# Weight rows 68 KB apart in DRAM instead of 64 KB: a gap of 4 KB behind every row of a load

## The chip, the cores and the metric

The kernel runs on one core of one Trainium2 chip. The metric is the device time of one execution in microseconds. Times are medians of several runs. The profile comes from one further execution.

## The reference

One decode step of a transformer block for 8 sequences: layer norm, attention over the last 1024 cached positions (32 query heads, 4 key and value heads, head size 128), a residual sum, a second layer norm, a gated MLP (1024 to 3584 to 1024), and a second residual sum. All in float32.

```python
q = (_layernorm(x) @ wq)                       # [8, 1, 32*128]
k = k_cache[:, :, Sk - W:, :]                  # W = 1024 of Sk = 4096, each head used by 8 query heads
v = v_cache[:, :, Sk - W:, :]
h = x + (softmax(q @ k.T * Dh ** -0.5) @ v) @ wo
n = _layernorm(h)
h2 = h + (gelu(n @ w_gate) * (n @ w_up)) @ w_down
```

With one token for each sequence nearly all the work is to bring the weights and the two caches from DRAM to the core: 111.2 MB, each byte used once.

## The kernel before

The host packs weights and caches into one flat DRAM array, `weights`. It is made of 20 parts, one for each load. A part is a matrix of 128 rows, one for each partition, and a row holds all that this partition gets from the load. Eleven parts have rows of 64 KB (16384 float32: the two halves of wq, K, V, wo, and three of the gate and up matrices), three have rows of 32 KB, two of 16 KB, one of 8 KB, one of 4 KB, and two of 2 KB. Rows and parts lie one behind the other without a gap, so the distance between two rows of a part is the length of a row.

In SBUF the array `w` has two buffers of 64 KB a partition, `wbuf[0]` and `wbuf[1]`, filled in turn. The function `load` (the issue stands on L186) starts loads 0 to 15 from the SP queue; the list `flow` gives each one's buffer, its offset and its source. Load k waits until TensorE has finished the products that read the same buffer before (`pe(...)`, two stages back). The last four loads, the `tail` (rows of 8, 4, 2 and 2 KB), go through `move` (L83). All 20 loads are on the one SP queue, in that order.

TensorE runs a loop of 13 half stages: `transposes` (L132, eight 128x128 transposes) and `products` (L146, 32 matmuls of 128x512 for each half stage's two halves), then some short matmuls for the end (L450, L463, L478). `products` first waits for the semaphore that says that the buffer's load has landed. Softmax, layer norm and sums run on VectorE, ScalarE and GpSimd between the stages. The 64 KB result goes out in two stores from the SP and ACT queues.

Of the kernel before, what the change touches and what calls it, by code (L numbers as in the profile page):

```python
# [8 lines left out]
P = 128  # L9
# [12 lines left out]
BUF = 32 * N  # L22
HALF = BUF // 2
WIN = 160


LATE = (5, 6, 4)
# [6 lines left out]
class Flow:  # L34
# [38 lines left out]
    def run(self, engine, make, *waits, mark=True):  # L73
        ins = self.start(engine, make, waits)
        if not mark:
            return None
        self.done[engine] += 1
        ins.then_inc(self.own[engine], 1)
        return self.own[engine], self.done[engine]
# [6 lines left out]
    def go(self, engine, sem, n, *waits):  # L86

        self.start(engine, lambda e: e.sem_inc(sem, n), waits)


def decode_block(nc, x, flow, tail, outs):
# [5 lines left out]
    def sb(name, *shape):  # L97
        return nc.alloc_sbuf_tensor(name, list(shape), F32).ap()
# [8 lines left out]

    st = [sb(f"st{i}", P, 2 * NQ * WIN) for i in range(2)]
    tin = sb("tin", P, NC * P)
# [9 lines left out]
    def pe(it, step):  # L119
        return steps, 6 * it + 1 + ("t0", "a0", "a1", "t1", "b0", "b1").index(step)  # L120
# [5 lines left out]
    def take(sem, n):  # L126
        t.wait_ge(sem, n).then_inc(sem, -n)  # L127
# [7 lines left out]
    def products(i, half):  # L135
# [4 lines left out]
        for n in range(4 * NQ):  # L140
            c, j = divmod(n, NQ)
            if (i, half, n) == (0, 1, 8):
                take(ready[i], 1)
            s0 = (half * NQ + j) * WIN + 32 * c
            w0 = half * HALF + (c * NQ + j) * N
# [54 lines left out]
    tin_zero = run("gpsimd", lambda e: e.memset(tin, 0.0))  # L200
    qz = [sb(f"qz{hf}", P, NQ * WIN) for hf in range(2)]
    zero = [run("gpsimd", lambda e, q=q: e.memset(q, 0.0)) for q in qz]
# [62 lines left out]
    for hf in range(2):  # L265
# [9 lines left out]
        for s in range(2):  # L275
# [6 lines left out]
            st[hf].rearrange("p (k n) -> p k n", k=2),  # L282
            qz[hf].unsqueeze(1).to_broadcast([P, 2, NQ * WIN])), tok, pe(0, end))
        go("gpsimd", ready[hf], 3 - hf, fill)
# [282 lines left out]
```

## Time and profile before

| What | Value |
|---|---|
| Time, median of 3 runs | 264.27 us (264.25 to 264.36) |
| The profiled execution's own time | 264.18 us |
| Its span, first to last instruction | 262.9 us |
| TensorE busy (matmuls) | 153.1 us, 58% of the span |
| VectorE, ScalarE, GpSimd busy | 35.0, 16.5, 15.8 us |
| Packets of the SP queue | 3024, 111.22 MB, 98.3% of 16 DMA engines' span |
| Read from DRAM | 111.18 MB |

The time of an execution is a little longer than the span (264.18 against 262.9 us), since what lies before the first and behind the last instruction counts as well. The DMA share is the time for which the core's 16 DMA engines had a packet in work, taken together.

### The profile page before, as it was taken

Reading aid. Unit: us, or ns where it says so; the run is one execution under the profiler, and the core shown is the slowest. Engines: PE = TensorE matmul, PEld = TensorE weight load, DVE = VectorE, ACT = ScalarE, POOL = GpSimd, SP = SyncE. Lnnn points to the kernel's source line nnn. Section 1 sums busy time; section 2 is a strip of 40 time slices with the busy share of each in tenths; the row PEclk is TensorE's granted clock in tenths of the full one; section 3 lists DMA queues with packets and bytes.
Section 4 is the critical chain, followed back from the end, with each engine's and each line's share of the span. In section 5 each row is a group of like instructions: output and inputs, shape, how many; then the busy total and the mean of one; then the engine's idle time right before and its main releaser. Section 6 shows DMA issues by size and latency. Waiting matters only on the chain. (4 is left out here: it accounts for less than half of the span.)

```text
span 262.9 us, 2330 instructions
## 1 busy us (share of the span) xinstructions
PE 153.1 (58%) x992; PEld 51.6 (20%) x992; DVE 35.0 (13%) x79; ACT 16.5 (6%) x25; POOL 15.8 (6%) x31
## 2 busy tenths in 40 slices
PE   0024945816926617937728908529919509966696
PEld 0021221211211112212212202122212202312112
DVE  0220010000030110040220010730011300131012
ACT  1000000000040110000000000200200000010000
POOL 5020010010000000010020000020000200001000
PEclk9999995986995975975956995955977956999799
DMA  8998997999899899989999997999999799999995
GB/s 319 484 449 349 479 479 329 469 479 449 349 479 479 369 429 479 449 349 479 479 399 399 479 459 339 479 479 399 399 479 479 319 464 414 439 439 399 431 419 207
DMA packets 3200, 111.31 MB, mean 423 GB/s; under 512 B 368, under 2 KB 624, under 8 KB 1024
## 3 DMA queue, kind: packets, MB, share of 16 engines
q1 hardware_dynamic: 3024, 111.22, 98.3%
q10 hardware_dynamic: 176, 0.10, 0.1%
HBM read 111.18 MB, written 0.13 MB: 423 GB/s over the span
## 5 line engine op out<-in xcount | busy, mean ns | idle before, releaser
L146 PE MATMUL big<-w,st 128*32 128x512 f32 x832 | 133.9, 728 | 72.9 <-PEq L127 69.6
L146 PEld LDWEIGHTS big<-w,st 128*32 128x32 f32 x832 | 36.7, 130 | 161.9 <-issue 159.4
L132 PE MATMUL tp<-ident,tin 128*128 128x128 f32 x104 | 16.7, 312 | 34.2 <-PEq L127 34.2
L132 PEld LDWEIGHTS tp<-ident,tin 128*128 128x128 f32 x104 | 13.2, 159 | 44.5 <-issue 44.5
L255 POOL COPY st<-ot 128x256 f32<-128x256 f32 x8 | 2.9, 402 | 77.6 <-DVE ot L334 77.6
L293 DVE TENSOR_REDUCE nmax<-big 128x1 f32<-128x1024 f32 x2 | 2.4, 1224 | 29.9 <-PE big L146 29.9
L246 POOL COPY st<-xt 128x1024 f32<-128x1024 f32 x2 | 3.0, 1524 | 51.7 <-DVE xt L241 51.7
L271 DVE TENSOR_TENSOR tin<-big,q 128x512 f32<-128x512 f32 x2 | 1.4, 692 | 32.3 <-PE big L146 32.3
L319 DVE TENSOR_TENSOR o<-big,o 128x512 f32<-128x512 f32 x2 | 1.4, 692 | 30.7 <-PE big L146 30.7
L281 POOL COPY st<-qz 128x1280 f32<-128x1280 f32 x2 | 2.5, 1256 | 35.1 <-DVE qz L276 35.1
L255 POOL COPY st<-at 128x256 f32<-128x256 f32 x6 | 2.6, 466 | 31.5 <-DMA w<-weights 25.5
L270 ACT COPY q<-big 128x512 f32<-128x512 f32 x2 | 1.2, 586 | 35.5 <-PE big L146 35.5
L443 DVE TENSOR_TENSOR d<-big,d 128x512 f32<-128x512 f32 x2 | 1.4, 692 | 14.9 <-PE big L146 14.9
L405 DVE TENSOR_TENSOR gs<-big,gs 128x512 f32<-128x512 f32 x1 | 0.7, 692 | 19.1 <-PE big L146 19.1
L318 ACT COPY o<-big 128x512 f32<-128x512 f32 x2 | 1.2, 586 | 31.5 <-PE big L146 31.5
L255 POOL COPY st<-xt 128x256 f32<-128x256 f32 x2 | 1.3, 661 | 30.1 <-DVE us L377 30.1
L295 ACT ACTIVATE tin<-big,nmax 128x1024 f32<-128x1024 f32 x2 | 2.2, 1114 | 12.8 <-DVE nmax L293 12.8
L295 ACT ACT_TABLE_LOAD x1 | 1.3, 1283 | 25.1 <-DVE nmax L293 25.1
L348 DVE TENSOR_TENSOR y<-big,y 128x512 f32<-128x512 f32 x1 | 0.7, 692 | 16.1 <-PE big L146 16.1
L226 ACT ACT_TABLE_LOAD x2 | 2.6, 1283 | 1.9 <-POOL ident L197 1.9
L373 DVE TENSOR_TENSOR gs<-big,gs 128x512 f32<-128x512 f32 x1 | 0.7, 692 | 14.7 <-PE big L146 14.7
L404 ACT COPY gs<-big 128x512 f32<-128x512 f32 x1 | 0.6, 586 | 30.6 <-PE big L146 30.6
(75 smaller groups left out, 44.6 us busy)
## 6 DMA issues: line engine op xcount, KB each, us to landing
w<-weights SPq DMA_DIRECT2D x3, 4096.0 KB, 22.8
w<-weights SPq DMA_DIRECT2D x2, 2048.0 KB, 23.8
w<-weights SPq DMA_DIRECT2D x1, 1024.0 KB, 24.3
w<-weights SPq DMA_DIRECT2D x1, 512.0 KB, 25.2
w<-weights SPq DMA_DIRECT2D x2, 256.0 KB, 25.5
w<-weights SPq DMA_DIRECT2D x11, 27.3
out<-o_fin SPq DMA_DIRECT2D x1, 64.0 KB, 1.6
out<-o_fin ACTq DMA_DIRECT2D x1, 64.0 KB, 1.6
```

Source lines behind the costliest of these rows:

```text
L132: ins = t.transpose(tp[:, i * P:(i + 1) * P], tin[:, i * P:(i + 1) * P], ident)
L146: ins = t.matmul(out[32 * j:32 * j + 32, :], st[i][:, s0:s0 + 32], wbuf[i][:, w0:w0 + N], start=(c == 0), stop=(c == 3))
L226: tok = run("scalar", lambda e: e.activation(sd, ve, AF.Sqrt), tok)
L246: fill = run(engine, lambda e: e.tensor_copy(windows(i), half.unsqueeze(2).to_broadcast([P, 2, NQ, 4 * 32])), tok, *clear)
L255: tok = run(engine, lambda e: e.tensor_copy(windows(i)[:, k, 2 * e2:2 * e2 + 2].rearrange("p h (c m) -> p h c m", m=32), s[:, e2].unsqueez ...
L270: tok = run("scalar", lambda e: e.copy(q_sb, w0), pe(0, ("a0", "b0")[hf]))
L271: tok = run("vector", lambda e: e.tensor_add(tin[:, 0:N], w1, q_sb), tok, pe(0, end), pe(0, ("t0", "t1")[hf]))
L281: fill = run("gpsimd", lambda e: e.tensor_copy(st[hf].rearrange("p (k n) -> p k n", k=2), qz[hf].unsqueeze(1).to_broadcast([P, 2, NQ * WIN ...
L293: tok = run("vector", lambda e: e.tensor_reduce(out=nmax, in_=s_ps, axis=AX.X, op=ALU.max, negate=True), pe(1, ("a1", "b1")[hf]))
L295: p_ok = run("scalar", lambda e: e.activation(tin, s_ps, AF.Exp, bias=nmax, accum_out=tot), tok, pe(1, ("t0", "t1")[hf]))
L319: tok = run("vector", lambda e: e.tensor_add(o_sb, big[hf][:, N:2 * N], o1), tok, pe(2, ("a1", "b1")[hf]))
L443: tok = run("vector", lambda e: e.tensor_add(d0, ya[:, k], d0), tok, pe(6, f"a{k}"))
```

## The change

Behind every row of every part the host puts 4 KB of zeros (`GAP` is 1024 float32). The source of a load then has a row step of n + 1024 elements and reads n of each. 64 KB rows begin 68 KB apart, 32 KB rows 36 KB, 2 KB rows 6 KB. The array grows by 20 x 128 x 4 KB, some 10.5 MB, which no load reads. The loads, their number, order, sizes, destinations and waits stay, and so does every instruction on every engine; source lines behind the new constant move down by two.

```diff
+GAP = 1024
...
-        "weights": np.concatenate([p.reshape(-1) for p in parts]),
+        "weights": np.concatenate([np.pad(p, ((0, 0), (0, GAP))).reshape(-1) for p in parts]),
...
     for p in parts:
-        srcs.append(aps["weights"][at:at + p.size].rearrange("(p n) -> p n", p=P))
-        at += p.size
+        n = p.shape[1]
+        rows = aps["weights"][at:at + P * (n + GAP)].rearrange("(p n) -> p n", p=P)
+        srcs.append(rows[:, 0:n])
+        at += P * (n + GAP)
```

## Rows read from the trace of the kernel before

**Rows 1.** The page, part 1: busy time, share of the span, instructions.

```profile
PE 153.1 (58%) x992; PEld 51.6 (20%) x992; DVE 35.0 (13%) x79; ACT 16.5 (6%) x25; POOL 15.8 (6%) x31
```

**Rows 2.** The page, parts 2 and 3: DMA queue: packets, MB, share of 16 engines.

```profile
DMA  8998997999899899989999997999999799999995
q1 hardware_dynamic: 3024, 111.22, 98.3%
q10 hardware_dynamic: 176, 0.10, 0.1%
HBM read 111.18 MB, written 0.13 MB: 423 GB/s over the span
```

**Rows 3.** The page, part 6: DMA issues, KB each, median us to landing.

```profile
w<-weights SPq DMA_DIRECT2D x3, 4096.0 KB, 22.8
...
w<-weights SPq DMA_DIRECT2D x11, 27.3
out<-o_fin SPq DMA_DIRECT2D x1, 64.0 KB, 1.6
```

**Rows 4.** The chain that ended last, in order of time: start, us, what.

```profile
233.38 0.33 SPq L83
...
233.76 25.23 DMA w<-weights
258.98 0.04 issue
...
260.57 0.06 PE tp L478 x2
...
260.96 0.27 ACT o_fin L482
```

**Rows 5.** DMA view of 5.6 to 215.0 us: packets, MB, share of 16 engines.

```profile
q1 hardware_dynamic: 1536, 90.18, 99.5%
```

**Rows 6.** DMA view of 24.2 to 43.5 us, 64 KB rows.

```profile
q1 hardware_dynamic: 144, 8.39, 100.3%
```

**Rows 7.** DMA view of 178.9 to 198.3 us, 64 KB rows.

```profile
q1 hardware_dynamic: 144, 8.39, 99.9%
```

**Rows 8.** DMA view of 215.2 to 244 us, 32 KB rows.

```profile
DMA packets 432, 12.58 MB, mean 437 GB/s; under 512 B 48, under 2 KB 48, under 8 KB 48
q1 hardware_dynamic: 432, 12.58, 101.5%
```

**Rows 9.** Windows at the start: length, engines' busy us, clock, DMA share, GB/s.

```profile
0.00:1.70 1.70, 0.00 (x0) 0.00 (x0) 0.00 (x0) 0.00 (x0) 1.10 (x7) 1.00 0.00 0
1.70:2.40 0.70, 0.00 (x0) 0.00 (x0) 0.29 (x1) 0.52 (x1) 0.70 (x2) 1.00 4.18 1404
```

**Rows 10.** DMA view of 0 to 4.6 us.

```profile
q1 hardware_dynamic: 16, 1.05, 66.8%
```

**Rows 11.** DMA view of 254.8 to 258.6 us: rows of 8, 4 and 2 KB.

```profile
DMA packets 353, 1.53 MB, mean 404 GB/s; under 512 B 32, under 2 KB 32, under 8 KB 253
q1 hardware_dynamic: 353, 1.53, 99.3%
```

## The prediction

> **What bounds the kernel now.** I read the page's busy times first. TensorE, the busiest engine, works for 153.1 of 262.9 us [rows 1]; nothing there fills the span. The DMA rows do: the SP queue's packets kept 16 engines busy for 98.3% of the span, and the 40 slices show no gap before the last one [rows 2]. (A slice counts a packet where it starts, so its digit wavers between 7 and 9.) So the kernel is one stream of packets from end to end.
>
> The chain of waits looks different at first. Its longest piece is a load that TensorE released at 233.38 us and that landed 25.23 us after its issue [rows 4]. That is no cost of TensorE. The four loads issued there are the smallest of all, and they need so long because the queue in front of them was full. The same is seen on the eleven 8 MB loads: the median one lands 27.3 us after its issue [rows 3], while its own packets take 19.4 us (below). Loads are thus issued some 8 us before their turn, and a wait for a buffer stops no DMA engine.
>
> What is one packet? Of the 3024, each of 20 loads and one store has 144 (21 x 144 = 3024): 128 rows and 16 small ones, one for each engine (three loads show 384 rows and 48 packets under 512 B [rows 8]). A row of 64 KB is therefore one packet, one contiguous read of one row. Between 5.6 and 215.0 us 90.18 MB, that is 1376 such rows, took 99.5% of 16 engines [rows 5]: 0.995 x 209.4 x 16 / 1376 = 2.423 us a row, or 65,536 B / 2.423 us x 16 = 433 GB/s. Eight rows for each engine make 19.4 us a load. Single loads agree: 1.003 x 19.3 x 16 / 128 = 2.420 us in an early one [rows 6], 0.999 x 19.4 x 16 / 128 = 2.423 us in a late one [rows 7]. A row's time stays the same to 3 ns through the whole span, whichever array is read and whatever TensorE does beside it.
>
> **What the change does, part by part.** It adds and removes no instruction, no DMA, no wait, and no byte that is read. It changes one thing: where each of 2560 rows begins in DRAM. Each engine has 8 rows of each load, 160 in all, and 88 of these are 64 KB long. The question is whether a row's 2.423 us hangs on the distance to the next.
>
> The trace holds one comparison of that kind, since in this array the distance between rows is the length of a row. The 32 KB rows lie 32 KB apart: 1.015 x 28.8 x 16 / 384 = 1.218 us each [rows 8]. Two of them take 2.436 us against 2.423 us for one of 64 KB, so a row costs 13 ns of its own and the rest goes by bytes, at the same rate at either distance (rounding leaves about 2 ns). If a distance of 64 KB made reads collide in DRAM more than one of 32 KB, the longer rows would be dearer for each byte, and they are not. A rate this even also speaks for a limit in the DMA engines rather than in DRAM. I therefore cost the change at 0 ns a row. What hides a slightly slower or faster DRAM read is that limit; were it not there, each ns on a long row would be worth 88 ns at the end.
>
> The Trainium skill has a rule about just this change. Its page "DMA: Bandwidth & Descriptors", section "Latency and other measured facts", reports that HBM copies lose rate when the row pitch is a large power of two (207 GB/s at 512 KiB, 103 at 4 MiB), and that padding the pitch by 4 KB brought back the full 214 GB/s; it advises to pad. No run here has such a pitch: its smallest is eight times ours, and [rows 5, 8] show no loss at 64 KB. The same page, section "Where 436 GB/s comes from", gives 435.2 GB/s as the limit of the ports into SBUF; the 433 GB/s of [rows 5] lie 0.5% below it. By that page alone padding could shorten the stream by 0.5% of 257 us at most, an estimate of 1.4 us.
>
> The bounds of this unknown cost come from the rows. Below: all long rows as quick as in the quickest load that I looked at, 3 ns x 88 = 0.26 us gained. The first row of each engine, which is dearer, is the other thing that could be gained: the first 16 packets took 0.668 x 4.6 x 16 / 16 = 3.07 us each [rows 10], 0.65 us over the rest. Above: a row that no longer begins at a multiple of 64 KB pays its own 13 ns a second time: 88 x 13 ns = 1.1 us, or 2.1 us if all 160 rows pay.
>
> The sum, of the profiled execution. The first packets start behind 1.7 us [rows 9]. The first rows' extra is 0.65 us. 111.2 MB at 433 GB/s are 256.8 us. By bytes this is 106 rows of 64 KB for each engine, with the 13 ns of each; the other 54 of 160 rows add 54 x 13 ns = 0.7 us. That gives 259.9 us for the last load's end, and the last matmuls, which use it, stand at 260.57 us in the chain [rows 4]. Behind them come a copy of 0.27 us and a store of 1.6 us to landing [rows 3, 4]; some 0.4 us between these pieces are not in my sum. So the stream accounts for the span of 262.9 us, and no term of it moves. The predicted time is that of the profiled execution, 264.18 us, plus nothing: **264.2 us**, 0.03% under the median of the runs, 264.27 us.
>
> **The rivals.**
>
> *Padding frees the start.* Nearly all engines begin together (0.7 us x 1404 GB/s are 15 packets [rows 9]), on rows whose addresses differ by multiples of 64 KB; if these first reads collide in DRAM and drift apart afterwards, then the 0.65 us are the collision, and a distance of 68 KB takes it away: 263.5 us. For it: later rows cost 2.42 us at the same distance, so something is special about the first. Against it: any first read waits for its data while nothing is under way to cover that, and such a delay stays at every distance; the trace of before does not tell it from a collision. More than 0.53 us of the 0.65 would have to go for a gain that can be told from none.
>
> *Collisions slow the whole stream, and padding lifts it.* This is the skill's rule as a mechanism here. The rows allow only the 0.26 us between the quickest load and the mean, 263.9 us, which cannot be told from no change; for more, a limit would have to lie in DRAM that costs 64 KB and 32 KB rows the same, and nothing shows one. By the page's 435.2 GB/s it would be 262.8 us.
>
> *Each row gets dearer*, the case on the other side. Rows now start 4 KB off a 64 KB border, cross such a border in the middle, and no longer follow one another in DRAM. If each long row pays one further row cost, the time is 264.2 + 1.1 = 265.3 us, and with all rows 266.3 us. It is slower by what can be told from 0.53 / 88 = 6 ns a long row on, a quarter of a percent of 2.423 us; against it stands that the reads seem to wait for the engines, so DRAM may lose a little before it shows.
>
> *The change does not leave the packets as they are*: a strided source is cut into smaller pieces than a contiguous one. The shortest rows show the price: 404 GB/s at a share of 99.3% [rows 11], or 407 GB/s for engines that are always busy. At that rate 111.2 MB take 273 us in place of 257, and the time is about 280 us. Rows are packets already now, so there is no reason for another cut.
>
> **How the numbers follow.** A measurement of this kernel can tell a change of about 0.2%, 0.53 us, from none. No term moves: 0.86. Start freed, or the stream lifted by more than the rows suggest: 0.06 together, faster. Rows dearer by 6 ns and more: 0.07; smaller packets: 0.01; both slower. So faster 0.06, same 0.86, slower 0.08. The range goes from 263.5 us (all of the start's 0.65 us gained) to 265.3 us (one further row cost on each long row). It leaves out some 0.07: the far ends of the last two rivals and a stream lifted beyond the rows.
>
> **What would show it.** Right: the SP queue again with 3024 packets and 111.22 MB, a long row at 2.42 us between 5.6 and 215 us, 32 KB rows at 1.22 us, the first 16 packets near 3.07 us, and TensorE waiting for loads as before. The start rival would show as first packets of less than 2.6 us with all else shifted earlier by half a microsecond. The dearer rows would show as 2.429 us and more for a row, with loads landing later by 50 ns more each. A different count of packets would show another cut. The forecast is wrong if DRAM has a limit just above 433 GB/s that these rows do not reach and the new distance moves it below; nothing in the trace of before can exclude that.

## The result: slower by 0.19%, all of it lost in the first load

The change takes 264.86 us (median of 22 runs, 264.63 to 265.25), the kernel before 264.47 us beside it (22 runs, 264.13 to 264.89). The medians are 0.39 us apart. The ratio is 1.0019 with a 95% interval of 1.0013 to 1.0025, which makes it 0.5 us slower. The forecast was no change; 264.86 us lies in the range of 263.5 to 265.3 us, but the move is real and was not forecast. It is about as large as the 0.53 us that I had called the least that can be told from none.

The profiled execution of the change takes 264.84 us and its span is 263.5 us, 0.6 us more than before. Its page first, busy times and DMA queues (packets, MB, share of 16 engines):

```profile
PE 153.2 (58%) x992; PEld 52.6 (20%) x992; DVE 35.0 (13%) x79; ACT 16.5 (6%) x25; POOL 15.8 (6%) x31
...
q1 hardware_dynamic: 3024, 111.22, 98.2%
q10 hardware_dynamic: 176, 0.10, 0.1%
HBM read 111.18 MB, written 0.13 MB: 422 GB/s over the span
```

The packets and bytes are the same, and TensorE's matmuls take the same time to 0.1 us [rows 1, 2]. Its chain in order of time:

```profile
232.99 0.33 SPq L85
...
233.36 26.21 DMA w<-weights
259.57 0.04 issue
...
261.17 0.05 PE tp L480 x2
...
261.56 0.27 ACT o_fin L484
```

The loads that this chain follows land 0.59 us later than in [rows 4] (259.57 against 258.98 us), and everything behind them keeps its distance. So the time went into the stream of packets. The DMA view of the stretch from 5.6 to 215.0 us:

```profile
q1 hardware_dynamic: 1537, 90.24, 99.6%
```

That is 0.996 x 209.4 x 16 / 1377 = 2.423 us for a row of 64 KB, the same as in [rows 5]. From 24 us on no difference shows; this line of the view of 24 to 215 us is the same, digit for digit, in the trace of the kernel before and of the change:

```profile
q1 hardware_dynamic: 1408, 82.84, 100.2%
```

What is left is the time ahead of 24 us. TensorE's first matmuls on the first load, in the timeline (start, us, what; idle time before), of the kernel before:

```profile
23.03 7.54 PE L146 MATMUL big<-w,st 128*32 128x512 f32 x40 [7.04 <-PEq L127]
```

and of the change:

```profile
23.65 6.60 PE L148 MATMUL big<-w,st 128*32 128x512 f32 x34 [7.04 <-PEq L129]
```

They start 0.62 us later, which is the whole difference. Inside the first load there are two places to look at: the DMA views of 0 to 4.6 us (the 16 packets that start first) and of 7 to 9.4 us (the 16 that start third). Of the change:

```profile
q1 hardware_dynamic: 16, 1.05, 69.4%
...
q1 hardware_dynamic: 16, 1.05, 104.9%
```

Of the kernel before, 7 to 9.4 us:

```profile
q1 hardware_dynamic: 16, 1.05, 100.8%
```

The third rows take 1.049 x 2.4 = 2.52 us, against 2.42 us. The 16 first rows take 0.694 x 4.6 = 3.19 us each, against 3.07 us before [rows 10], but this mean does not tell the kernels apart: it is 3.15 us in e2_all_but_first below, which has no gap in load 0, and 3.09 us in e1_first_only, which has.

The mean of the 16 engines hides the main part, since a load has landed only when the last of its 16 semaphore steps has come (between 22.22 and 22.75 us for load 0 of the kernel before). The view has no row for single engines, so here are times worked out from the packets in the traces, in us from the span's start: when the slowest of the 16 first rows ended, how long the third rows took in the mean, when load 0 had landed, and how much later that is than the first column.

```
run                  slowest first row   third rows   load 0 landed   between
before                     5.35             2.418          22.75        17.40
after                      5.82             2.518          23.36        17.54
e11_change_again           5.66             2.560          23.25        17.59
e1_first_only              5.81             2.529          23.37        17.56
e7_pitch_96k               5.66             2.522          23.23        17.57
e0_before_again            5.46             2.533          23.03        17.57
e2_all_but_first           5.35             2.418          22.69        17.34
e3_zeros_behind            5.59             2.418          22.96        17.37
e4_shift_4k                5.30             2.418          22.67        17.37
e5_pitch_128k              5.32             2.418          22.71        17.39
e6_gap_256b                5.37             2.418          22.75        17.38
```

In the change the slowest first row ends 0.47 us later than in the kernel before, and what follows adds 0.14 us. The table holds the first runs of the next section too. One execution says little about a first row: runs without gaps in load 0, or with gaps of 64 or 0.25 KB, range from 5.30 to 5.59 us, those with 4 or 32 KB gaps from 5.66 to 5.82 us. Taken over all launches that were profiled, the restarts below among them, the mean is 5.40 us without gaps in load 0 or with gaps of 64 KB (nine launches) and 5.77 us with 4 or 32 KB (five), a difference of 0.37 us.

### The profile page after: what moved, and what is told of

The parts are those of the page before. It is cut to its first block, busy times and chain, and to the rows that moved or that the text cites. A ratio compares the mean times of both kernels' runs of the same rounds, so it can differ in the third digit from the quotient of the medians.

```text
span 263.5 us, 2330 instructions
## 1 busy us (share of the span) xinstructions
PE 153.2 (58%) x992; PEld 52.6 (20%) x992; DVE 35.0 (13%) x79; ACT 16.5 (6%) x25; POOL 15.8 (6%) x31
## 2 busy tenths in 40 slices
DMA packets 3200, 111.31 MB, mean 422 GB/s; under 512 B 368, under 2 KB 624, under 8 KB 1024
## 3 DMA queue, kind: packets, MB, share of 16 engines
q1 hardware_dynamic: 3024, 111.22, 98.2%
## 5 line engine op out<-in xcount | busy, mean ns | idle before, releaser
L134 PE MATMUL tp<-ident,tin 128*128 128x128 f32 x104 | 17.4, 323 | 34.8 <-PEq L129 34.8
L134 PEld LDWEIGHTS tp<-ident,tin 128*128 128x128 f32 x104 | 14.0, 166 | 45.2 <-issue 45.2
```

Source lines behind the costliest of these rows:

```text
L134: ins = t.transpose(tp[:, i * P:(i + 1) * P], tin[:, i * P:(i + 1) * P], ident)
```

## The experiments

Two theories at the start. *Start theory*: the loss is made while load 0 runs and hangs on where the rows of that load are. *Dearer rows*: every row costs some ns more; the even rows from 24 us on speak against it, but one profile is one execution. Two rivals more: the array's size or place, and chance. The code cuts below show the lines that differ from the change; the lines that give each load its own gap (`GAPS`) and put zeros ahead of and behind the array (`LEAD`, `TAIL`) are left out (...).

**The kernel before, again** (e0_before_again, no edit).

> The kernel before, unchanged, as the measure of what two series of one kernel differ by. Start theory (the 0.5 us are lost while the first load runs, and lie in where its rows are): ratio 1.000 within 0.0007; in the profile the first load lands near 22.75 us and the 16 packets of the third row take 2.418 us each, as before. Chance theory (the first load's delay differs from execution to execution, and the profile of the change caught a bad one): here too the first load may land anywhere from 22.7 to 23.4 us.

Measured: 264.47 us beside 264.29 us for the same kernel in the same series, ratio 1.0009 (1.0000 to 1.0018). Two series of one kernel thus differ by 0.09%, by up to 0.2% within the interval. The profile shows one thing in which executions of one kernel differ: third rows of 2.533 us and a load that lands at 23.03 us, with a slowest first row that is not late, at 5.46 us. The slow third rows are therefore not made by the gaps alone. The late first row is the part that the change has and this run has not.

**Gaps in load 0 alone, and in all loads but load 0** (e1_first_only, e2_all_but_first).

```diff
-GAP = 1024
+GAPS = [1024] + [0] * 19
...
```

```diff
-GAP = 1024
+GAPS = [0] + [1024] * 19
...
```

> 4 KB gaps in load 0 alone, the 19 others without gaps. Start theory: the whole loss, +0.4 to +0.6 us (ratio 1.0015 to 1.0023), first load landing near 23.3 us. Dearer rows (each row of every load costs a few ns more): +0.05 us, no difference. Size theory (the array is larger, or lies elsewhere in DRAM): no difference, since it grows by 0.5 MB of 111 MB.

> 4 KB gaps in loads 1 to 19, none in load 0. Start theory: no difference (ratio 0.9995 to 1.0007), first load landing near 22.75 us. Dearer rows: nearly the whole loss, +0.45 us. Size theory: the whole loss, +0.5 us.

Measured: load 0 alone gives 264.84 us, ratio 1.0020 (1.0011 to 1.0029), the whole loss. The 19 other loads give 264.36 us, ratio 1.0002 (0.9993 to 1.0011). The profile of the first run has the first load's lateness (23.37 us), and the windows of the second show none: the third rows (7 to 9.4 us) and the rows of 5.6 to 215.0 us, with gaps from load 1 on:

```profile
q1 hardware_dynamic: 16, 1.05, 100.8%
...
q1 hardware_dynamic: 1536, 90.18, 99.5%
```

2.42 us for both. Dearer rows is refuted: 2432 of 2560 rows with a gap behind them cost nothing that the interval would show (0.3 us for all of them together).

**Zeros behind the array** (e3_zeros_behind: no gaps, 10.5 MB of zeros behind the last part).

```diff
-GAP = 1024
+GAPS = [0] * 20
+LEAD, TAIL = 0, 2621440
...
```

> No gaps; 10.5 MB of zeros behind the last part, so that the array has the size it has with the gaps. Start theory and dearer rows: no difference. Size theory: +0.5 us.

Measured: 264.40 us, ratio 1.0003 (0.9994 to 1.0012). The size is not it.

**What about the place of load 0's rows?** Four kernels, each against the series' kernel before at 264.43 us.

```diff
-GAP = 1024
+GAPS = [0] * 20             # e4: every row 4 KB later, 64 KB apart
+LEAD, TAIL = 1024, 0
...
+GAPS = [16384] + [0] * 19   # e5: load 0, rows 128 KB apart
...
+GAPS = [64] + [0] * 19      # e6: load 0, rows 64.25 KB apart
...
+GAPS = [8192] + [0] * 19    # e7: load 0, rows 96 KB apart
...
```

> No gaps, but 4 KB of zeros ahead of the first part: every row begins 4 KB off its old place, 64 KB from its neighbour. Three readings of the loss in load 0. Border theory (a first row that does not begin at a multiple of 64 KB of the array is read later): the whole loss, +0.4 to +0.6 us, first matmul near 23.6 us. Strided theory (a source with gaps takes longer to start than one without): no difference, first matmul near 23.0 us. Phase theory (what counts is how the 16 first rows stand to one another modulo 64 KB): no difference.

> Load 0 alone has gaps, of 64 KB, so its rows lie 128 KB apart and each begins at a multiple of 64 KB. Border theory: no difference. Strided theory: the whole loss, +0.4 to +0.6 us. Phase theory: no difference, since all rows stand at the same place modulo 64 KB.

> Load 0 alone has gaps, of 256 B, so 64 KB rows lie 64.25 KB apart. Border theory and strided theory: the whole loss, +0.4 to +0.6 us. Phase theory: less than the whole loss, since the 128 rows spread over only 32 KB modulo 64 KB, in steps of 256 B.

> Load 0 alone has gaps, of 32 KB: rows lie 96 KB apart and stand at two places modulo 64 KB. Border theory: about half of the rows are off a border, and the slowest engine has such rows, so up to the whole loss. Strided theory: the whole loss. Phase theory: a loss, if two places are already worse than one; else none.

Measured: e4 264.35 us, ratio 0.9999 (0.9990 to 1.0008); e5 264.40 us, 0.9999 (0.9990 to 1.0008); e6 264.31 us, 0.9995 (0.9986 to 1.0004); e7 264.68 us, 1.0009 (1.0000 to 1.0018). Rows off a 64 KB border are free (e4): the border theory falls, and with it the place that my slower rival gave for its price. A gap as such is free (e5): the strided theory falls. What remains is how the rows stand to one another modulo 64 KB: where all stand at one place (e4, e5), or each only 0.25 KB behind the one before (e6), nothing is lost; at two places, 32 KB apart (e7), the first row is late (5.66 us). How far the rows spread does not decide it, since those of e6 spread over 32 KB as well. The time of e7 shows nothing by itself: its ratio is that of e0, which has no edit at all. Which of a load's 128 rows are the 16 first ones, the traces do not tell.

**Many starts in one execution** (e8_restart, e9_restart_gaps, e10_restart_mixed). In these loads 2 to 11 wait until half of the products on the load before are done, so that the stream runs dry ten times. Nothing of the computation is left out.

```diff
-        clear = pe(min(k // 2, 5) - 1, ("a1", "b1")[i]) if k <= 12 else pe(
+        clear = pe((k - 1) // 2, ("a0", "b0")[(k - 1) % 2]) if k < 12 else pe(
+            4, "b1") if k == 12 else pe(
...
+GAPS = [0] * 20      # e8
...
+GAPS = [1024] * 20   # e9
...
+GAPS = [0, 0, 0, 1024, 0, 2048, 4096, 8192, 16384, 64, 256, 15360] + [0] * 8   # e10
```

> No gaps; loads 2 to 11 wait until TensorE has done half of the products on the load before, so that the stream of packets runs dry and starts anew ten times. It is the baseline for the next two: some 4 to 8 us later for each restart. Each restart shows a first row of near 3.1 us, if that is a price of any start; if it is a price of the program's first read alone, later first rows take 2.42 us.

> The same restarts with 4 KB gaps in all loads. Cold stream theory (whenever the stream starts from rest, rows 68 KB apart come later by up to 0.5 us on the slowest engine): 10 x 0.3 to 0.5 us on top of the 0.5 us, that is 3 to 6 us over the restarts without gaps. Program start theory (only the first read after the launch is sensitive): 0.4 to 0.6 us over the restarts without gaps.

> The same restarts; loads 0, 1, 2 and 4 without gaps, and loads 3 and 5 to 11 with gaps of 4, 8, 16, 32, 64, 0.25, 1 and 60 KB. Cold stream theory: the slowest engine's first row ends later after the restarts with 4, 8, 16, 60 KB (and somewhat with 32 KB) than after those with 0, 64 and 0.25 KB, by 0.2 to 0.5 us. Program start theory: all ten restarts look alike.

Measured: 344.70 us without gaps, 353.09 us with them, 350.27 us mixed. The kernel with gaps is now 8.4 us slower than the one without. The first is 1.3034 (1.3012 to 1.3055) times the kernel before, the second 1.3340 (1.3285 to 1.3395). The DMA view gives the median time from issue to landing over the eleven loads of 8 MB; without gaps and then with them:

```profile
w<-weights SPq DMA_DIRECT2D x11, 21.8
```

```profile
w<-weights SPq DMA_DIRECT2D x11, 22.4
```

So a load is 0.6 us longer in the median, and not at the launch alone. The program start theory is refuted. The packets of the nine restarts of 64 KB rows (loads 2 to 10) again: us from the restart's first packet until the slowest of the 16 first rows ended, here with three more runs that are told of next:

```
gap     run              nine restarts                                          mean
0       e8_restart       3.84 3.50 3.53 3.78 3.54 3.56 3.64 3.56 3.64           3.62
64 KB   e12_restart_64k  3.57 3.64 3.43 3.67 3.54 3.59 3.74 3.69 3.72           3.62
0.25 KB e14_restart_256b 3.59 3.79 3.59 3.77 3.76 3.66 3.58 3.76 3.73           3.69
1 KB    e13_restart_1k   4.14 3.90 3.76 3.76 3.94 3.99 3.36 3.50 3.79           3.79
4 KB    e9_restart_gaps  3.64 4.24 4.15 4.27 3.72 3.98 4.19 4.23 3.59           4.00
```

With 4 KB, six of the nine starts are later than every start without gaps. In e10 the starts with gaps of 4, 8, 16, 32 and 1 KB end their slowest first row at 4.15, 3.98, 4.07, 4.12 and 4.16 us, those with none, 64 KB and 0.25 KB at 3.58, 3.56, 3.49 and 3.51 us. (Load 11, with 60 KB gaps, has rows of 32 KB and does not compare.) With 4 KB the slowest first row is later by 0.38 us in the mean, and by the same 0.38 us the whole load is longer, on average from the first packet to the last (20.53 and 20.91 us). In both 16.91 us pass from the end of the slowest first row to the load's last packet: what the first row loses stays lost.

Nine times 0.38 us are 3.4 of the 8.4 us. From the first packet of load 2 to the last of load 10 e9 needs 6.5 us more (246.2 against 239.7 us); the 3.1 us beside the loads lie between the end of one load and the start of the next, where TensorE does half of the products. The granted TensorE clock differs a little between the two executions (the view of cores, e8 and then e9):

```profile
core 0: 343.9 us, clock 0.757
```

```profile
core 0: 351.7 us, clock 0.748
```

The traces show that those 3.1 us go with the clock. Here are the stretches of e9 between loads 4 and 5 and between loads 6 and 7, with the same 38 matmuls (length, engines' busy us, granted clock as a share of full speed and so a mix of its two levels 0.5 and 1, DMA share, GB/s):

```profile
126.65:134.82 8.17, 7.42 (x38) 1.89 (x39) 0.00 (x0) 0.59 (x1) 0.00 (x0) 0.60 0.03 8
183.78:190.69 6.91, 6.14 (x38) 1.59 (x39) 0.00 (x0) 0.59 (x1) 0.00 (x0) 0.71 0.00 0
```

Length times granted clock is 4.9 us in both, and 4.9 to 5.0 us in each of the eight such stretches of e8 and of e9. The lengths run from 6.8 to 7.0 us in e8 and from 6.6 to 8.2 us in e9, where two stretches have a clock of 0.60. So of the 6.5 us only 3.4 us are the first rows'. Why e9 was granted less clock there is not shown. In the two profiled executions the spans differ by 7.8 us; the other 1.3 us lie before load 2 and behind load 10.

**Which distances** (e12_restart_64k, e13_restart_1k, e14_restart_256b: the restarts with `GAPS = [16384] * 20`, `[256] * 20`, `[64] * 20`).

> Restarts as before, gaps of 64 KB in all loads (long rows 128 KB apart). Phase theory (a loss only where rows stand at different places modulo 64 KB): slowest first rows end 3.6 us after the restart on average, as without gaps, and the time is near 345 us. Any-gap theory: 4.0 us and near 352 us.

> Restarts as before, gaps of 1 KB in all loads (long rows 65 KB apart). Phase theory: 3.9 to 4.1 us on average and 349 to 353 us, since 1 KB a row already puts the rows at 64 different places. If the loss needs steps of 4 KB: 3.6 us and near 345 us.

> Restarts as before, gaps of 0.25 KB in all loads. If the loss grows with how far the rows spread: 3.6 to 3.7 us on average and near 345 us. Any-gap theory, and a phase theory in which any difference counts: 4.0 us and 349 to 353 us.

Measured, one execution each: 343.37 us at 64 KB, 347.76 us at 1 KB, 344.06 us at 0.25 KB. The first is as quick as without any gap: the any-gap theory falls for good. The means of the slowest first row rise with the step, 3.62, 3.69, 3.79, 4.00 us for 0, 0.25, 1 and 4 KB, but only the last stands clear of the scatter: the starts run from 3.50 to 3.84 us without gaps, from 3.58 to 3.79 us with 0.25 KB and from 3.36 to 4.14 us with 1 KB. The single restart at 1 KB in e10 ended its slowest first row at 4.16 us, the launch of e13 at 5.31 us, as if there were no gap, and from 4 to 32 KB e10 shows no further rise. My expectation for the mean at 1 KB (3.9 us or more) was too high. Whether 1 KB costs something between nothing and the whole is not settled; that places differ is not enough, since 0.25 KB puts the rows at different places too.

**The change, again** (e11_change_again, no edit).

> The change, unchanged, for a second profile. If the loss is the pitch's, the first load lands near 23.4 us again, with its slowest first row ending near 5.8 us and its third rows at 2.52 us. If the profile of the change caught a bad start, it may land near 22.8 us.

Measured: 264.70 us, first matmul at

```profile
23.54 6.93 PE L148 MATMUL big<-w,st 128*32 128x512 f32 x34 [7.04 <-PEq L129]
```

and its packets as in the table at the top: slowest first row at 5.66 us, third rows at 2.560 us. Both parts of the loss come again.

## Why the prediction was wrong

- **What bounds the kernel**: right. One stream of packets, whose lateness of 0.59 us came out at the end almost to the digit.
- **0 ns for a row while the stream runs**: right, and shown by e2_all_but_first. 2.42 us is the price of a 64 KB row at 64 and 68 KB alike. The comparison of 32 KB with 64 KB rows [rows 5, 8] pointed the same way, but with some luck: both distances are powers of two, and about 68 KB it said nothing.
- **The first rows**: this is the step that failed. I had seen that they are dearer by 0.65 us [rows 10], and that a start from rest may be sensitive to where the rows are. But I let that count in one direction: "the other thing that could be gained", a rival with 263.5 us. Its other sign, rows 68 KB apart that come later at the start than rows 64 KB apart, had no term, no price and no chance. I had also read the first rows as a mean of 16 engines, and the mean does not show the loss. The runs showed in its place that of the 16 first rows the slowest, which decides when the load lands, ends 0.47 us later in this profile and 0.38 us later a start over nine restarts. I had written that the 0 holds only while the engines' own limit hides the reads; the start may be the place where that cover is missing, but no run shows that this is the reason.
- **The slower rival** gave the sign and 0.53 us as the point from which it tells, but by a charge on every long row. That mechanism is refuted (e2, e4). That the measured 264.86 us lay below its bound of 265.3 us is luck.
- **The rule of the Trainium skill** ("DMA: Bandwidth & Descriptors", "Latency and other measured facts": pad the row pitch by 4 KB) spoke for a gain at pitches from 512 KiB on. At 64 KB no run shows one: the stream runs at 433 GB/s with and without a gap, and the padding of 4 KB makes the start slower.
- **Packets**: 3024 and 111.22 MB, as forecast; no other cut.

Open stay two things. What in the chip makes first reads at different places modulo 64 KB slower was not seen; the runs show at which distances it was seen (68, 72, 80 and 96 KB, and in part of the starts 65 KB) and at which not (64, 64.25 and 128 KB), not why. And the slow third rows: all five executions profiled with 4 or 32 KB gaps in load 0 have them (after, e11, e1, e7, e9), but so have e0 and e10, which have no gap there, while ten others (no gap there, or one of 0.25, 1 or 64 KB) have none. They go with a "between" of 17.54 to 17.63 us in place of 17.34 to 17.40 us, some 0.2 us; why they come at times to a kernel without gaps was not found out, and part of the measured 0.5 us is probably theirs. No distance that was tried starts quicker than rows without gaps, so no run points to a version that beats the kernel before.

## What to carry to other kernels

Here a stream of transfers that runs at a steady 2.42 us for every row hid where its rows lie, and its start did not. When costing a change to addresses, cost the first row of the slowest engine by itself and with both signs. Where each load starts from rest, such a detail counts once for each start (0.38 us here), and restarts made on purpose are a good magnifying glass for an effect of 0.2%, read from the packets and not from the time: more than half of the 8.4 us between e8 and e9 did not come from the first rows of the restarts.

## What was unexpected in the hardware

Rows at equal places modulo 64 KB (distances of 64 and 128 KB) were the quickest to start, 3.62 us, not the slowest, and spreading them by 4 KB a row made the slowest first row end 0.38 us later. Each of the nine restarts in the middle of e8 made first rows take some 3.1 us for 2.42 us (3.01 to 3.13 us in the mean of 16 engines), as at the beginning of the execution (3.09 us), so this is no price of the first read after the launch alone.
